# W1 loaded right behind batch 0 and scaled by three engines, batch 1's attention moved between the first MLP matmuls, g turned on TensorE

## The chip, the cores and the metric

One core of one Trainium2 chip runs the whole program. The metric is the device time of one execution in microseconds (us). The kernel before took 349.22 us as the median of three runs (346.89 to 353.25). Times below are medians of runs; positions inside a run are microseconds from the start of the profiled span, which is about 2 us shorter than the run's time.

## The reference, cut to what matters

```python
# 8 batches, 8 heads, 576 rows, 64 columns a head
A  = softmax(q @ q_or_k_landmarks); Bm = softmax(q_lm @ k_lm^T); C = softmax(q_lm @ k^T)   # 32 landmarks
Z  = Bm^T / (norm1 * norminf)
for _ in range(6):
    Z = 2 * Z - Z @ Bm @ Z              # "Newton's steps"
x  = (A @ Z @ C @ v)                    # attention's output, as rows of 512
xn = (x - mean) / sqrt(var + 1e-6) * g_ln
out = x + relu(xn @ w_ch1) @ w_ch2      # MLP, 512 -> 2048 -> 512
```

The kernel takes the g of the normalisation into W1: each row of W1 is multiplied by one element of g when it is brought to fp16. The rows of all batches are cut into 36 blocks of 128 and 9 groups of four blocks; the MLP runs group by group.

## The kernel before: the parts that matter here

All transfers go through one queue, in program order: batch 0's q, k, v, then g, batch 1's q and k, W1, batch 1's v, W2, and later the other batches. W1's and W2's fp32 pieces and the attention's output blocks share one pool of 16 buffers:

```python
xpool = ctx.enter_context(tc.tile_pool(name="xpool", bufs=16))
def scale_w1(i):                       # W1 in pieces of 256 columns
    for c in range(KCH):
        if c == 0: act(o, i_, AF.Copy, scale=g_sb[:, c:c + 1])      # ScalarE
        else:      pool.tensor_scalar(out=o, in0=i_, scalar1=g_sb[:, c:c + 1], ...)   # GpSimd
def fetch_w2():
    for m in range(MCH + 6):
        if m < MCH:
            w2_stg[m] = xpool.tile([P, DM], FP32, name="w2stg", tag="xblk")
            keep(nc.sync.dma_start(out=w2_stg[m][:], in_=moe_w_ch2[ts(m, P), :]))
        if m >= 6:
            pool.tensor_copy(out=w2_16[:, m - 6, :], in_=w2_stg.pop(m - 6)[:])
def x_of(j):                           # the buffer of output block j
    if j not in x_blk:
        x_blk[j] = xpool.tile([P, DM], FP32, name="xblk", tag="xblk")
    return x_blk[j]
```

The MLP is a generator; `fill(n)` issues its next n units (one to three matmuls each) between the steps of an attention. `a0` and `a1` are the attentions of batches 0 and 1. In the kernel before, batch 1's q and k steps run between Newton's steps of batch 0, and its later steps between the MLP's first matmuls:

```python
run(a0, a1, a0); warm(2, 256)          # warm: idle matmuls that keep TensorE's clock up
run(a0, a1, a0); warm(2, 256)
run(a0, a1, a0, a0)
scale_w1(0); run(a1); fill(1); run(a0); scale_w1(1); ...
for _ in a0: pass                      # the rest of batch 0's rows
run(a1); fill(10); cast_v(1)
fetch_w2()                             # W2 after batch 0's rows
...
for i, _ in enumerate(a1):
    fill(5 if i < 8 else 6); settle()
    cast_and_load(pairs[0], pairs[1])
    if 3 <= i < 11: pairs[0].next_job()    # VectorE's preparation of batches 2 and 3
```

The names in the profile: psb are the landmark scores, psn Newton's products, pszc the product after the last step, psy the output rows, xblk the blocks, psxt and xnT the turned activations, psh and pso the two MLP matmuls, natv the attention's values. Where a milestone is needed below I use four: the first psh, batch 1's pszc, the second half of the psb of batches 2 and 3 ("second psb"), and the end.

The softmax here doesn't subtract the row's maximum and nothing guards it: scores larger than these inputs give would overflow.

Of the kernel before, what the change touches and what calls it, by code (L numbers as in the profile page):

```python
# [9 lines left out]
FP16 = mybir.dt.float16  # L10
# [6 lines left out]
P = 128  # L17
# [3 lines left out]
def kernel(  # L21
# [67 lines left out]
    def load_qk(b):  # L89
        for u in range(U):  # L90
            raw[b]["q", u] = load(q, b, u, nc.sync)
            raw[b]["k", u] = load(k, b, u, nc.sync)
# [30 lines left out]
    keep(nc.sync.dma_start(out=g_sb[:], in_=moe_g_ln.rearrange("(c p) -> p c", p=P)))  # L123
# [6 lines left out]

# [56 lines left out]
    load_qk(1)  # L187
    for u in range(U):
        for nm in ("q", "k"):
            cast_qk(1, u, nm, pool)  # L190

    w1_16 = wpool.tile([P, KCH, HID], FP16, name="w1_16")
    w2_16 = wpool.tile([P, MCH, DM], FP16, name="w2_16")
    w1_src = moe_w_ch1.rearrange("(c p) f -> p c f", p=P)
    xpool = ctx.enter_context(tc.tile_pool(name="xpool", bufs=16))

    W1N = 256
    w1_stg = {}



    def load_w1(i):
        for half in range(2):
            stg = xpool.tile([P, DM], FP32, name="w1stg", tag="xblk")
            keep(nc.sync.dma_start(
                out=stg[:].rearrange("p (c f) -> p c f", c=2),
                in_=w1_src[:, 2 * half:2 * half + 2, ts(i, W1N)]))
            w1_stg[i, half] = stg

    def scale_w1(i):  # L210
        for c in range(KCH):
            o, i_ = w1_16[:, c, ts(i, W1N)], w1_stg[i, c // 2][:, ts(c % 2, W1N)]
            if c == 0:
                act(o, i_, AF.Copy, scale=g_sb[:, c:c + 1])
            else:
                pool.tensor_scalar(out=o, in0=i_, scalar1=g_sb[:, c:c + 1],
                                   scalar2=0.0, op0=ALU.mult, op1=ALU.add)

    for i in range(HID // W1N):
        load_w1(i)  # L220
# [463 lines left out]
    def by_act(j):  # L684
        return 4 <= j < 8 or 8 <= j < 28 and j % 2 == 0
# [3 lines left out]
    def block_done(j):  # L689
# [3 lines left out]
        if g == 0:  # L693
            center_by_act(j)
            later.append(lambda: stats(j))
        elif g == 1:
            later.append(lambda: center_by_act(j))
        else:
            if by_act(j):
                later.append(lambda: stats_by_act(j))  # L700
            else:
                stats(j)
            later.append(lambda: center(j) if g <= mlp_at[0] + 1
                         else uncentered.setdefault(g, []).append(j))
# [27 lines left out]
    def center_by_act(j):  # L732
# [5 lines left out]
        if by_act(j):  # L738
            junk = mxn.tile([P, DM], FP16, name="junk", tag="junk", bufs=1)
            act(junk[:], x_blk[j][:], AF.Square, bias=negm[:],  # L740
                accum_out=mvgs[g][:, u, 1:2])
# [53 lines left out]
    def mlp():  # L795
        for g in range(NGRP):
            mlp_at[0] = g
            hT = mhT.tile([P, MCH, 512], FP16, name="hT", tag="hT")
            if g == 0:
                for u in (0, 2):  # L800
# [4 lines left out]
                    for m0 in range(0, MCH, 2):  # L805
# [3 lines left out]
                        if u == 0 and m0 < MCH - 6:  # L809
                            scale_w1(m0 // 2 + 3)  # L810
# [63 lines left out]
    def run(*who):  # L874
        for a in who:
            next(a)

    warm(80, 64)
    for _ in range(4):
        run(a0)  # L880
        warm(3, 256)
    run(a0)
# [4 lines left out]
    warm(4, 256)  # L887
    run(a0)
    warm(2, 256)
    run(a0)  # L890
    warm(2, 256)
    run(a0, a1, a0)
    warm(2, 256)
    run(a0, a1, a0)
    warm(2, 256)
    run(a0, a1, a0, a0)
    scale_w1(0)
    run(a1)
    fill(1)
    run(a0)  # L900
    scale_w1(1)
    fill(1)
    scale_w1(2)
    fill(4)
    run(a0)
    fill(4)
    for _ in a0:
        pass
    run(a1)
    fill(10)  # L910
    cast_v(1)
    fetch_w2()
    run(a1)
    fill(16)
# [12 lines left out]

    for i, _ in enumerate(a1):
        fill(5 if i < 8 else 6)
        settle()  # L930
        cast_and_load(pairs[0], pairs[1])
        if 3 <= i < 11:
            pairs[0].next_job()
    for _ in range(3):
        pairs[0].next_job()
# [48 lines left out]
```

## Time and profile before

| | before |
|---|---|
| time, us | 349.22 (346.89 to 353.25) |
| span of the profiled run | 346.7 |
| TensorE busy | 323.3, 93% |
| VectorE, ScalarE, GpSimd busy | 46%, 49%, 36% |
| first psh / batch 1's pszc / second psb | 29.22 / 54.58 / 74.17 |

The page's rows of busy tenths show where there is room. Each digit is 8.7 us; 9 means 90% or more.

```profile
PE 323.3 (93%) x3818; PEld 166.4 (48%) x3818; DVE 158.7 (46%) x341; ACT 168.6 (49%) x328; POOL 125.5 (36%) x199
...
PE   8875979879889999999999999999999999999994
...
PEclk9999999989999999999999999999999999999998
DMA  7999999999982281171012101210130031022023
```

Apart from the last slice, TensorE is below 9 only in the first twelve, 104 us, and the DMA engines are full in the same stretch. The clock is full but for two slices. After those twelve nothing but TensorE's matmuls counts.

This is how TensorE reaches its first MLP matmul in the kernel before (its timeline: start, duration, what, number of instructions, and in brackets the idle time before it with what ended that):

```profile
20.06 0.43 PE L73 MATMUL pss<-pm,nat 128*128 128x64 f16 x9 [1.49 <-issue]
...
22.85 0.24 PE L73 MATMUL pszc<-st,bm 32*32 32x64 f16 x8
...
29.22 1.03 PE L73 MATMUL psh<-xnT,w 128*128 128x256 f16 x8 [0.52 <-DVE xnT L67]
```

Waiting on "issue" is waiting on nothing that the profile can name.

### The profile page before, as it was taken

What the parts mean: (1) busy time and instruction counts of PE and PEld (TensorE: products, weight loads), DVE (VectorE), ACT (ScalarE), POOL (GpSimd) and SP (SyncE); (2) the same over time, 40 slices, a digit from 0 to 9 for tenths busy, and PEclk for the clock granted to TensorE, in tenths of its full rate; (3) what the DMA queues carried; (4) which work ended last, traced back from release to release, by engine and by line L of the source; (5) the groups of instructions that cost most, each with busy time, mean ns of one, the idle gap of its engine ahead of it and who ended that gap; (6) DMA issues with size and microseconds to landing.
All of it is one profiled execution on the core that took longest, in us unless ns stands there. A gap on an engine that the chain in (4) does not pass through costs nothing.

```text
span 346.7 us, 8948 instructions
## 1 busy us (share of the span) xinstructions
PE 323.3 (93%) x3818; PEld 166.4 (48%) x3818; DVE 158.7 (46%) x341; ACT 168.6 (49%) x328; POOL 125.5 (36%) x199
## 2 busy tenths in 40 slices
PE   8875979879889999999999999999999999999994
PEld 7553744435433545554445444544444454444441
DVE  2645629885499753346777402337850010020011
ACT  4359844943544595045738750465146226415600
POOL 2488878999953498047023000003120010000000
PEclk9999999989999999999999999999999999999998
DMA  7999999999982281171012101210130031022023
GB/s 274 357 353 362 344 404 369 233 384 317 236 281 91 62 260 47 32 201 32 2 30 64 31 2 42 55 30 2 34 84 6 15 77 32 0 62 61 0 54 69
DMA packets 21528, 46.72 MB, mean 135 GB/s; under 512 B 3056, under 2 KB 7152, under 8 KB 21488
## 3 DMA queue, kind: packets, MB, share of 16 engines
q1 hardware_dynamic: 21488, 46.15, 43.6%
q8 instruction: 30, 0.49, 0.6%
q14 instruction: 10, 0.08, 0.1%
HBM read 36.70 MB, written 9.44 MB: 133 GB/s over the span
## 4 chain that ended last, share of the span: by engine, by line
PE 75%; DVE 7%; DMA 7%; ACT 6%; issue 2%; SPq 1%; POOL 0%; DVEq 0%
PE psh L73 35%; PE pso L73 30%; DMA w1stg<-in_moe_w_ch_dram 4%; DMA g_sb<-in_moe_g_ln_dram 3%; PE pscv L73 3%; ACT xn L67 2%; PE psy L73 2%; PE psxt L77 2%; DVE st L67 2%; DVE xblk L67 2%; PE psn L73 1%; DVE xT L67 1%; ACT junk L67 1%; PE psea L73 1%; PE psec L73 1%
## 5 line engine op out<-in xcount | busy, mean ns | idle before, releaser
L73 PE MATMUL pso<-w,hT 128*128 128x512 f16 x576 | 137.6, 381 | 0.0
L73 PE MATMUL psh<-xnT,w 128*128 128x512 f16 (+1 forms) x640 | 133.7, 358 | 2.9 <-DVE xnT L67 1.2
L67 ACT ACTIVATE hT<-psh 128x512 f16<-128x512 f32 x144 | 85.3, 597 | 54.5 <-PE psh L73 54.3
L73 PEld LDWEIGHTS <-w 128*128 128x128 f16 x640 | 59.7, 98 | 60.6 <-issue 2.3
L73 PEld LDWEIGHTS <-hT 128*128 128x128 f16 x576 | 53.9, 98 | 55.7 <-issue 2.1
L67 DVE SCALAR_TENSOR_TENSOR ot<-pso,rstd,xblk 128x512 f32<-128x512 f32 x36 | 27.0, 749 | 107.7 <-PE pso L73 107.7
L67 ACT COPY xnT<-psxt 128x512 f16<-128x512 f16 x32 | 18.7, 584 | 59.1 <-PE psxt L77 59.0
L67 POOL CAST nat<-stg 128x1152 f16<-128x1152 f32 x28 | 31.8, 1147 | 5.1 <-DMA stg<-in_k_dram 1.8
L67 DVE TENSOR_TENSOR xblk<-psy,rcpd 128x512 f32<-128x512 f32 (+1 forms) x40 | 27.6, 691 | 1.8
L67 POOL TENSOR_SCALAR xn<-xblk,negm 128x512 f16<-128x512 f32 x18 | 12.5, 694 | 35.2 <-PE psxt L77 34.1
L67 DVE SCALAR_TENSOR_TENSOR st<-st,psn 128x384 f16<-128x384 f16 (+3 forms) x30 | 13.5, 450 | 24.2 <-PE psn L73 24.2
L67 POOL TENSOR_SCALAR xn<-xblk,mvg 128x512 f16<-128x512 f32 x10 | 6.9, 695 | 45.8 <-PE psxt L77 28.3
L67 POOL CAST natv<-stg 128x1152 f16<-128x1152 f32 x16 | 17.9, 1151 | 11.8 <-DMA stg<-in_v_dram 11.8
L67 DVE STREAM_TRANSPOSE xT<-nat 128x576 uint32<-128x576 uint32 x24 | 18.4, 767 | 4.8 <-POOL nat L67 3.5
L67 POOL TENSOR_SCALAR negm<-mvg 128x1 f32<-128x1 f32 x18 | 3.5, 192 | 37.6 <-PE psy L73 23.9
L73 PE MATMUL psy<-zcbd,ea 128*128 128x260 f16 (+1 forms) x80 | 16.0, 277 | 1.2 <-ACT xT L67 0.6
L77 PE MATMUL psxt<-ident,xn 128*128 128x128 f16 x144 | 14.2, 222 | 2.1 <-ACT xn L67 1.6
L67 DVE TENSOR_REDUCE lmk<-xT 128x64 f16<-128x1152 f16 x12 | 16.1, 1341 | 0.1
L67 POOL TENSOR_TENSOR asum<-asum 128x256 f32<-128x256 f32 (+2 forms) x30 | 15.0, 501 | 2.3
L67 DVE BATCH_NORM_STATS2 st<-xblk 128x6 f32<-128x512 f32 x22 | 15.2, 689 | 0.6
L77 PEld LDWEIGHTS <-xn 128*128 128x128 f16 x144 | 10.9, 99 | 9.1 <-ACT xn L67 2.0
L67 DVE RECIPROCAL rcpd<-psy 128x8 f32<-128x8 f32 (+1 forms) x40 | 8.0, 201 | 11.1 <-PE psy L73 10.6
(99 smaller groups left out, 257.6 us busy)
## 6 DMA issues: line engine op xcount, KB each, us to landing
stg<-in_q_dram SPq DMA_DIRECT2D x16, 576.0 KB, 6.9
stg<-in_k_dram SPq DMA_DIRECT2D x16, 576.0 KB, 7.8
out_dram<-ot SPq DMA_DIRECT2D x72, 128.0 KB, 2.4
stg<-in_v_dram SPq DMA_DIRECT2D x10, 576.0 KB, 8.2
w1stg<-in_moe_w_ch_dram SPq DMA_DIRECT2D x16, 256.0 KB, 6.0
w2stg<-in_moe_w_ch_dram SPq DMA_DIRECT2D x16, 256.0 KB, 5.2
stg<-in_v_dram SPq DMA_DIRECT2D x12, 288.0 KB, 8.7
g_sb<-in_moe_g_ln_dram SPq DMA_DIRECT2D x1, 2.0 KB, 10.1
```

What stands on the lines that cost most here:

```text
L67: return lambda *args, **kw: keep(getattr(self.engine, op)(*args, **kw))
L73: keep(nc.tensor.matmul(o, l, r, start=start, stop=stop, tile_position=(rb, cb), skip_group_check=(skip or cb != 0)))
L77: keep(nc.tensor.matmul(o, i_, idn, is_transpose=True, tile_position=(0, 0)))
```

## The change

Its intent: the MLP should start earlier and then run without gaps. W1 is loaded right behind batch 0's data in pieces of 512 columns and scaled by GpSimd, VectorE and ScalarE between Newton's steps; batch 1's whole attention moves behind the MLP's start, one step between every few MLP units; g arrives in four rows of 512 bytes and is turned by one TensorE matmul; group 1's statistics go from ScalarE partly to VectorE. W2's loads move ahead of batch 0's rows, and nine blocks are named before them, so that the blocks have their buffers first.

```diff
-    keep(nc.sync.dma_start(out=g_sb[:], in_=moe_g_ln.rearrange("(c p) -> p c", p=P)))
+    keep(nc.sync.dma_start(out=g_rows[:], in_=moe_g_ln.rearrange("(c p) -> c p", p=P)))
-    load_qk(1)                       # and its casts; W1 behind it in pieces of 256 columns
+    for f in range(HID // DM):
         for c in range(KCH):
+            w1_stg[f, c] = stg = xpool.tile([P, DM], FP32, name="w1stg", tag="xblk")
+            keep(nc.sync.dma_start(out=stg[:], in_=moe_w_ch1[ts(c, P), ts(f, DM)]))
+    load_qk(1)
     load_v(1)
... by_act, block_done: statistics of groups 0 and 1
-        if g == 0:
+        if g == 0 and u % 2 == 0:
             center_by_act(j)
             later.append(lambda: stats(j))
-        elif g == 1:
-            later.append(lambda: center_by_act(j))
+        elif g == 0:
+            stats(j)
+            ... dve.tensor_scalar(out=xn_of[j][:], in0=x_blk[j][:], ..., op0=ALU.subtract)
... the order of steps
-    for _ in range(4):
+    for i in range(4):
         run(a0)
         warm(3, 256)
+        if i == 2:
+            TR(psg[:], g_rows[:], ident4[:])
+            dve.tensor_copy(out=g_sb[:], in_=psg[:])
...
+    scale(pool, (0, 3), (1, 3), (2, 0), (2, 1), (2, 3), (3, 0), (3, 1), (3, 3))
+    for it, on_dve in enumerate(((0, 0), (0, 1), None, (1, 0), (1, 1), None)):
+        run(a0) ; scale(dve, on_dve) ; scale(scalar, ...) ; warm(2, 256)
...
+    for j in range(9):
+        x_of(j)
+    fetch_w2()
     run(a0)                          # batch 0's rows: block 0, block 1
...
+    ahead = [2, 2, 2, 3, 4, 4, 7] + 6 * [5] + [5, 4, 5, 5, 5, 5]
     for i, _ in enumerate(a1):
-        fill(5 if i < 8 else 6)
+        fill(ahead[i])
         settle()
-        if 3 <= i < 11: pairs[0].next_job()
+        if i >= 9:  cast_and_load(pairs[0], pairs[1])
+        if i >= 12: pairs[0].next_job()
+    while pairs[0].jobs:
+        pairs[0].next_job(); fill(4); cast_and_load(pairs[0], pairs[1])
```

More of the change, by code (lines that the diff above doesn't have):

```diff
@@ L122 @@
     g_sb = wpool.tile([P, KCH], FP32, name="g_sb")
-    keep(nc.sync.dma_start(out=g_sb[:], in_=moe_g_ln.rearrange("(c p) -> p c", p=P)))
+    g_rows = wpool.tile([KCH, P], FP32, name="g_rows")
+    keep(nc.sync.dma_start(out=g_rows[:], in_=moe_g_ln.rearrange("(c p) -> c p", p=P)))
     zeros = const.tile([P, 256], FP16, name="zeros")
@@ L129 @@
     make_identity(nc, ident16)
+    ident4 = const.tile([KCH, KCH], FP32, name="ident4")
+    nc.vector.tensor_copy(out=ident4[:], in_=ident16[0:KCH, 0:KCH])
     pm16 = const.tile([P, 64], FP16, name="pm16")
@@ L184, with scale_w1 @@
                 dve.tensor_copy(out=t[:, :, D], in_=(mask4t if i in (3, 5) else mask4)[:])
-    load_qk(1)
-    for u in range(U):
-        for nm in ("q", "k"):
-            cast_qk(1, u, nm, pool)
     w1_16 = wpool.tile([P, KCH, HID], FP16, name="w1_16")
     w2_16 = wpool.tile([P, MCH, DM], FP16, name="w2_16")
-    w1_src = moe_w_ch1.rearrange("(c p) f -> p c f", p=P)
     xpool = ctx.enter_context(tc.tile_pool(name="xpool", bufs=16))
-    W1N = 256
     w1_stg = {}
-    def load_w1(i):
-        for half in range(2):
-            stg = xpool.tile([P, DM], FP32, name="w1stg", tag="xblk")
-            keep(nc.sync.dma_start(
-                out=stg[:].rearrange("p (c f) -> p c f", c=2),
-                in_=w1_src[:, 2 * half:2 * half + 2, ts(i, W1N)]))
-            w1_stg[i, half] = stg
-    def scale_w1(i):
-        for c in range(KCH):
-            o, i_ = w1_16[:, c, ts(i, W1N)], w1_stg[i, c // 2][:, ts(c % 2, W1N)]
-            if c == 0:
-                act(o, i_, AF.Copy, scale=g_sb[:, c:c + 1])
-            else:
-                pool.tensor_scalar(out=o, in0=i_, scalar1=g_sb[:, c:c + 1],
-                                   scalar2=0.0, op0=ALU.mult, op1=ALU.add)
-    for i in range(HID // W1N):
-        load_w1(i)
+    for f in range(HID // DM):
+        for c in range(KCH):
+            w1_stg[f, c] = stg = xpool.tile([P, DM], FP32, name="w1stg", tag="xblk")
+            keep(nc.sync.dma_start(out=stg[:], in_=moe_w_ch1[ts(c, P), ts(f, DM)]))
+    def scale_w1(f, c, engine):
+        o, i_ = w1_16[:, c, ts(f, DM)], w1_stg.pop((f, c))[:]
+        if engine is scalar:
+            act(o, i_, AF.Copy, scale=g_sb[:, c:c + 1])
+        else:
+            engine.tensor_scalar(out=o, in0=i_, scalar1=g_sb[:, c:c + 1],
+                                 scalar2=0.0, op0=ALU.mult, op1=ALU.add)
+    load_qk(1)
     load_v(1)
@@ L684, in by_act @@
     def by_act(j):
-        return 4 <= j < 8 or 8 <= j < 28 and j % 2 == 0
+        return 4 <= j < 28 and j % 2 == 0
     rstds = {}
@@ L692, in block_done @@
             mvgs[g] = mstat.tile([P, 4, 2], FP32, name="mvg", tag="mvg")
-        if g == 0:
+        if g == 0 and u % 2 == 0:
             center_by_act(j)
             later.append(lambda: stats(j))
-        elif g == 1:
-            later.append(lambda: center_by_act(j))
+        elif g == 0:
+            stats(j)
+            xn_of[j] = mxn.tile([P, DM], FP16, name="xn", tag="xn")
+            dve.tensor_scalar(out=xn_of[j][:], in0=x_blk[j][:], scalar1=mvgs[0][:, u, 0:1],
+                              scalar2=None, op0=ALU.subtract)
         else:
@@ L737, in center_by_act @@
         act(xn[:], x_blk[j][:], AF.Identity, bias=negm[:], scale=1.0)
-        if by_act(j):
-            junk = mxn.tile([P, DM], FP16, name="junk", tag="junk", bufs=1)
-            act(junk[:], x_blk[j][:], AF.Square, bias=negm[:],
-                accum_out=mvgs[g][:, u, 1:2])
     def center(j):
@@ L808, in mlp @@
                             yield True
-                        if u == 0 and m0 < MCH - 6:
-                            scale_w1(m0 // 2 + 3)
                         psh = psM.tile([P, 2, 256], FP32, name="psh", tag="pm")
@@ L872, with run, scale @@
     a0, a1 = attention((0,)), attention((1,))
-    def run(*who):
-        for a in who:
-            next(a)
+    def run(a):
+        next(a)
+    def scale(engine, *pieces):
+        for f, c in pieces:
+            scale_w1(f, c, engine)
     warm(80, 64)
-    for _ in range(4):
+    for i in range(4):
         run(a0)
         warm(3, 256)
+        if i == 2:
+            psg = psM.tile([P, KCH], FP32, name="psg", tag="pm")
+            TR(psg[:], g_rows[:], ident4[:])
+            dve.tensor_copy(out=g_sb[:], in_=psg[:])
     run(a0)
@@ L887 @@
     warm(4, 256)
+    scale(pool, (0, 3), (1, 3), (2, 0), (2, 1), (2, 3), (3, 0), (3, 1), (3, 3))
+    for it, on_dve in enumerate(((0, 0), (0, 1), None, (1, 0), (1, 1), None)):
+        run(a0)
+        if on_dve:
+            scale(dve, on_dve)
+        if it in (1, 3, 5):
+            scale(scalar, (it // 2, 2))
+        warm(2, 256)
     run(a0)
     warm(2, 256)
-    run(a0)
-    warm(2, 256)
-    run(a0, a1, a0)
-    warm(2, 256)
-    run(a0, a1, a0)
-    warm(2, 256)
-    run(a0, a1, a0, a0)
-    scale_w1(0)
-    run(a1)
+    for u in range(U):
+        for nm in ("q", "k"):
+            cast_qk(1, u, nm, pool)
+    cast_v(1)
+    for j in range(9):
+        x_of(j)
+    fetch_w2()
+    run(a0)
+    run(a0)
     fill(1)
+    scale(scalar, (3, 2))
+    fill(5)
     run(a0)
-    scale_w1(1)
-    fill(1)
-    scale_w1(2)
     fill(4)
     run(a0)
-    fill(4)
-    for _ in a0:
-        pass
-    run(a1)
-    fill(10)
-    cast_v(1)
-    fetch_w2()
-    run(a1)
-    fill(16)
+    settle()
+    run(a0)
     settle()
@@ L926, in cast_and_load @@
             (c if c.loads else after).next_load()
+    ahead = [2, 2, 2, 3, 4, 4, 7] + 6 * [5] + [5, 4, 5, 5, 5, 5]
     for i, _ in enumerate(a1):
-        fill(5 if i < 8 else 6)
+        fill(ahead[i])
         settle()
+        if i >= 9:
+            cast_and_load(pairs[0], pairs[1])
+        if i >= 12:
+            pairs[0].next_job()
+    while pairs[0].jobs:
+        pairs[0].next_job()
+        fill(4)
         cast_and_load(pairs[0], pairs[1])
-        if 3 <= i < 11:
-            pairs[0].next_job()
-    for _ in range(3):
-        pairs[0].next_job()
     counts = [[5, 5, 12, 12, 12, 12, 5, 5, 3, 3, 3, 3, 4] + 3 * [4] + 7 * [9]]
```

## The prediction

> **What bounds the kernel now.** I read the page's busy shares first (TensorE 93%, VectorE 46%), then the chain of work that ended last, then the engines' busy time in stretches of 5 us, then the order of instructions around each stretch where TensorE has gaps. From about 110 us to the end TensorE is full (the stretches show 9.7 to 10 of 10 us), so whatever the change does before 110 us reaches the end one to one, and nothing after it can absorb or add much. The early chain:
>
> ```profile
> 3.97 10.05 DMA g_sb<-in_moe_g_ln_dram
> 14.06 9.32 DMA w1stg<-in_moe_w_ch_dram
> 23.39 4.76 DMA w1stg<-in_moe_w_ch_dram
> 28.16 0.49 ACT w L67
> 28.65 1.00 ACT xT L67
> 29.65 0.64 ACT xn L67 x2
> ```
>
> The columns are start, duration, what. The chain says that W1 arrives late; this is what the change attacks. But the order of instructions shows a second arrival at the same moment: the first MLP matmul (psh) starts at 29.22 and its last releaser is the turned activation, 0.42 us at 28.74; W1's piece was scaled at 28.65. So W1 earlier alone buys about half a microsecond; the activation's own chain has to shorten too.
>
> The stretches (us; then PE, PEld, DVE, ACT, POOL busy, granted clock, DMA share, GB/s):
>
> ```profile
> 25.00:30.00 5.00, 2.90 (x38) 2.26 (x38) 2.88 (x7) 4.53 (x9) 4.61 (x11) 1.00 1.10 349
> 30.00:35.00 5.00, 3.27 (x29) 2.27 (x27) 2.64 (x7) 4.94 (x13) 4.23 (x8) 1.00 1.07 371
> 50.00:55.00 5.00, 3.24 (x43) 1.98 (x44) 4.37 (x7) 1.21 (x3) 4.04 (x4) 1.00 1.02 408
> 55.00:60.00 5.00, 5.00 (x26) 2.28 (x25) 4.84 (x10) 2.15 (x5) 4.09 (x4) 1.00 1.04 363
> 60.00:65.00 5.00, 4.59 (x43) 2.11 (x41) 4.93 (x10) 4.83 (x12) 4.61 (x7) 1.00 1.03 230
> 65.00:70.00 5.00, 4.11 (x47) 2.06 (x48) 3.85 (x6) 4.90 (x14) 4.69 (x8) 1.00 1.02 240
> 70.00:75.00 5.00, 2.44 (x57) 1.09 (x55) 4.31 (x9) 1.50 (x4) 4.31 (x5) 0.95 1.02 388
> 75.00:80.00 5.00, 5.00 (x129) 2.67 (x111) 3.99 (x12) 1.78 (x3) 4.60 (x8) 0.71 1.03 392
> ```
>
> ScalarE is full from 25 to 35; VectorE is nearly full from 50 to 75, and TensorE has holes there: that is the other limit. VectorE's groups from 50.6 to 74.2 name the work, and TensorE's waits from 29 to 75 its price:
>
> ```profile
> L67 DVE STREAM_TRANSPOSE xT<-nat 128x576 uint32<-128x576 uint32 x8 | 6.2, 770 | 3.5 <-POOL nat L67 3.5
> L67 DVE TENSOR_REDUCE lmk<-xT 128x64 f16<-128x1152 f16 x4 | 5.3, 1334 | 0.0
> L67 DVE TENSOR_REDUCE lmq<-xT 128x64 f16<-128x1152 f16 x2 | 2.7, 1348 | 0.0
> ...
> PE psn L73 <- DVE st L67: 2.1, 1, 2.1
> PE psb L73 <- DVE lmq L67: 2.0, 2, 1.2
> ```
>
> These 14 jobs prepare batches 2 and 3 (14.5 us with the two lmq transposes). TensorE's second half of their psb matmuls at 74.17 waits for the last of them.
>
> **What the Trainium skill says.** "DMA: Bandwidth & Descriptors", section "Queues, rings and completion order": each engine consumes a ring's descriptors in ring order. The trace agrees: all transfers come from one queue, batch 0's pieces land in order at 4.5, 6.0, 8.6, 10.1, 12.1 and 13.7 us, and g, issued at 3.97 just behind v, lands at 14.06. The section "Why a DMA increments its semaphore by 16 and not by 1" says that the number of engines follows from the slowest dimension, so g in four rows uses four engines instead of 16; no run here shows that yet. It means four larger descriptors, but still behind v in those rings. "VectorE: DVE Perf Modes", section "Mode 2×_2P — use both read ports for one tensor", gives fp32 tensor_scalar from SBUF two results a cycle, as for copies; the trace's cast of 1152 fp32 in 760 ns (0.66 ns each) agrees with a double rate.
>
> **The change part by part.**
>
> *W1 behind batch 0, in 2 KB rows.* Batch 0 ends at 13.7. A 262 KB piece at the trace's 350 to 400 GB/s takes 0.7 to 0.75 us: the 16 pieces land from about 14.4 to 25.5, instead of to about 31. GpSimd has 8 x 0.69 = 5.5 us instead of 24 x 0.48 = 11.5; ScalarE 4 pieces of about 0.65 instead of 8 x 0.49; VectorE 4 of about 0.4 (estimate from the cast), in the 0.4 to 0.5 us gaps that Newton's steps leave. W1 then gates nothing. Batch 1's q and k land behind it, at about 27.5 to 33, v at 36, and W2 to 46 or so, about as now because the bytes to there are the same.
>
> *g turned on PE.* The turn stands in TensorE's program order before the fourth q/k step, which now runs at 10.9. By the ring order g lands at about 13.3 to 13.7. So TensorE stands there 2.5 us. Of it 0.25 comes back, because batch 0's value product already waits that long for v. Newton then starts at about 18.3 instead of 15.96.
>
> *Batch 1 out of batch 0's way.* Newton's six steps and the next stage took 15.96 to 22.85 = 6.9 us, with one 2.4 us wait of VectorE in which TensorE did batch 1's work. Alone they take 6 x 0.87 = 5.2, some 5.4 with the scaling. The last product is then at 23.7 (now 22.85). Behind it: zcbd 1.2, psy and reciprocal, block 0 at +2.5, block 1 at +3.4, its statistics 0.8 and subtraction 0.4 on VectorE, turning and copying 0.8: first MLP matmul at +5.5, so about 29.2, against 29.22 now. Without the g wait it would be 26.8.
>
> *Batch 1 inside the MLP.* Its four q/k steps, now before 29, cost TensorE about 1.15 each with gaps, 4.6 us behind the MLP's start. The wait of its second step for a PSUM buffer that VectorE frees after group 0's late statistics costs some 2 us more. In exchange disappear most of the gaps between 29 and 53 (about 5 us in the windows: 1.7 in 30 to 35, 2.1 at 50 where a job stood before Newton's update). From the start to batch 1's last Newton step: 24.0 now, about 26.5 after. That step is at 53.2 now, and then at 53.3 (no g wait) to 56.
>
> *The jobs for batches 2 and 3.* Now they begin at 50.6, between Newton's steps; then only at the last one. VectorE has behind it jobs 14.5, five rows 5 x 0.9 = 4.5, zcbd 0.9, three outputs 2.2, plus new statistics for two blocks of group 1, 1.7: 24.1, some 22.6 with the overlap now seen (24 us of records in 22.4). So the psb at 74.17 moves to 76 to 78.6: 2 to 4.5 us later. It stands at nearly the same place in the MLP stream: 127 units of fill before it now (36 + 70 + 5 + 16), 126 after (10 + 83 + 28 + 5).
>
> *ScalarE's chain for group 1* (its 8 us from 60 to 68) goes: 4 x about 2.3 us become 2 x 1.7 on ScalarE and 3 us on GpSimd. That frees an engine that in this stretch is not the one TensorE waited for longest.
>
> *Later.* Between 74 and 110 TensorE idles about 3 us and lost 1.5 us to a clock of 0.71 in 75 to 80 (5 x 0.29). If it comes later to the same places, 1 to 2 us of this can go. Sum: +2 to +4.5, less 1 to 2: about +1.5 us by the working.
>
> **The rivals.** (1) *The intended gain.* g lands in time (four rows only, nothing in the rings ahead), the MLP starts at 26.8, and the filled gaps and the relieved ScalarE count in full: 11 us of TensorE gaps between 29 and 110 shrink to 5 or 6. Then 340 to 344. For it: the fill numbers look tuned to arrivals; ScalarE is 97% busy from 60 to 70 now. Against it: VectorE's 22 us of work before that psb. (2) *VectorE binds fully*, the g wait is full, and nothing is recovered: 353 to 356. (3) *Only trading*: start earlier, the same work moved behind it, all gaps alike: 348 to 350.
>
> **Range and chances.** My working gives 350.7; because the hand-set fill numbers speak for rival 1, I put it at 350.0. The time before itself spread from 346.89 to 353.25. Range 342.5 to 356. Faster by over 2% (below 342.2) 0.13, within 2% 0.73, slower (above 356.2) 0.14.
>
> **What would show it.** In the changed profile: g's landing and a wait of TensorE ahead of psg near 11 to 13.5; first psh near 29 (rival 1: under 27); W1's pieces all scaled before 27; TensorE nearly without gaps from 30 to 53; the first xT of batches 2 and 3 after 53 rather than 50.6; VectorE full from there and the second psb at 76 or later. I am wrong if g lands by 11, or if that psb comes before 73.

## The result

The changed kernel is correct and took 367.57 us (366.46 to 369.57, four runs) beside 348.58 us for the kernel before (346.89 to 353.25, four runs, of which the one of 353.25 counts as slow): a ratio of 1.0557, with a 95% interval of 1.0486 to 1.0627. It is 5.6% slower, where I had predicted 350.0 us and a range that ended at 356. A ratio here is the mean time of one kernel's fast runs over that of the other's fast runs of the same rounds, so it is not quite the ratio of the medians that I quote.

The page of the changed kernel, the rows that answer to those shown of before:

```profile
PE 327.0 (90%) x3825; PEld 168.5 (46%) x3825; DVE 163.8 (45%) x353; ACT 160.2 (44%) x306; POOL 123.3 (34%) x189
...
PE   7770569986889899999999999999999999999994
...
PEclk9685599999999999999999999999999999999999
DMA  7999997044997636316201300220022022022013
```

A slice is 9.1 us here. The fourth slice, 27 to 36 us, has a busy share of 0 on TensorE, and the clock is at 0.5 in it and in the next one. That hole was in no part of my prediction.

TensorE's timeline of the changed kernel shows the hole and the milestones:

```profile
12.95 0.24 PE L77 MATMUL psg<-ident,g_rows 4*128 4x4 f32 x1 [2.68 <-DMA g_rows<-in_moe_g_ln_dram]
...
26.75 1.20 PE L73 MATMUL psy<-zcbd,ea 128*128 128x260 f16 x4
39.29 0.61 PE L77 MATMUL psxt<-ident,xn 128*128 128x128 f16 x4 [11.34 <-ACT xn L67]
...
41.54 1.86 PE L73 MATMUL psh<-xnT,w 128*128 128x256 f16 x8 [0.52 <-DVE xnT L67]
...
68.05 0.24 PE L73 MATMUL psn<-st 32*32 32x64 f16 x8
69.42 0.24 PE L73 MATMUL pszc<-st,bm 32*32 32x64 f16 x8
...
91.11 0.22 PE L73 MATMUL psb<-lmk,lmq 32*32 32x32 f16 x6 [0.53 <-DVE lmq L67]
...
98.67 0.52 PE L73 MATMUL pscv<-natv,ecT 32*32 32x65 f16 x45 [1.30 <-issue]
...
104.32 0.20 PE L73 MATMUL pscv<-natv,ecT 32*32 32x65 f16 x1 [1.76 <-issue]
```

psy at 26.75 makes the first two output blocks. The activation made from them is turned only at 39.29, after 11.34 us. The releaser named is ScalarE's xn; ScalarE in turn waits for the block. So the question goes to VectorE, which writes the block. Its timeline:

```profile
27.56 0.21 DVE L67 RECIPROCAL rcpd<-psy 128x8 f32<-128x8 f32 x1 [0.47 <-PE psy L73]
37.03 0.69 DVE L67 TENSOR_TENSOR xblk<-psy,rcpd 128x512 f32<-128x512 f32 x1 [9.27 <-POOL w L67]
37.64 0.20 DVE L67 RECIPROCAL rcpd<-psy 128x8 f32<-128x8 f32 x1
37.93 0.69 DVE L67 TENSOR_TENSOR xblk<-psy,rcpd 128x512 f32<-128x512 f32 x1
```

The same two steps in the kernel before, without any wait between them:

```profile
24.39 0.21 DVE L67 RECIPROCAL rcpd<-psy 128x8 f32<-128x8 f32 x1 [0.36 <-PE psy L73]
24.68 0.69 DVE L67 TENSOR_TENSOR xblk<-psy,rcpd 128x512 f32<-128x512 f32 x1
```

In the changed kernel the reciprocal is done at 27.77, and the write of block 0 starts 9.27 us later. Nothing of its data is missing; its inputs are psy and that reciprocal. What released it is a GpSimd instruction that writes w. GpSimd's timeline tells which:

```profile
31.72 1.15 POOL L67 CAST nat<-stg 128x1152 f16<-128x1152 f32 x1 [0.36 <-DMA stg<-in_k_dram]
33.22 1.15 POOL L67 CAST natv<-stg 128x1152 f16<-128x1152 f32 x1 [0.36 <-DMA stg<-in_v_dram]
34.73 1.15 POOL L67 CAST natv<-stg 128x1152 f16<-128x1152 f32 x1 [0.35 <-DMA stg<-in_v_dram]
35.82 10.35 POOL L67 CAST w<-w2stg 128x512 f16<-128x512 f32 x16
```

W is here W2: the casts of its 16 pieces begin at 35.82, at 0.65 us each, behind the casts of batch 1's q, k and v, which follow their transfers. VectorE was released when the second cast was done, at about 37.0. A buffer that held a piece of W2 was handed to block 0. In the built program (seen in its allocations, not in a trace) block 0 has the same address as W2's second piece, and blocks 1 to 8 those of the next eight. The line `x_of(j)` for nine blocks ahead of `fetch_w2()` was written to prevent just this, and did not: naming a tile that nothing had written yet reserved nothing.

The stretches of 5 us (PE, PEld, DVE, ACT, POOL busy, granted clock, DMA share, GB/s) show what was running meanwhile:

```profile
25.00:30.00 5.00, 2.72 (x24) 1.02 (x24) 1.82 (x6) 0.00 (x0) 3.12 (x3) 0.53 1.05 395
30.00:35.00 5.00, 0.00 (x0) 0.00 (x0) 0.00 (x0) 0.00 (x0) 3.72 (x4) 0.50 1.05 389
35.00:40.00 5.00, 0.61 (x4) 0.34 (x4) 2.77 (x6) 2.06 (x4) 4.89 (x8) 0.50 1.05 387
```

TensorE, VectorE and ScalarE do nothing at all from 30 to 35. The clock stays at 0.50 until about 46 us, and the first eight psh matmuls took 1.86 us instead of 1.03. The Trainium skill's page "TensorE: Matmul & The Clock Gate", section "Part 1: The HAM clock gate (the "warmup" mystery)", says that TensorE runs at half its clock after about 3.4 us without work and needs as long of work to get it back. This trace agrees with that in part. The half clock lasted through the hole and ended at 45.8, 4.3 us after the first psh. But it had begun at 25.3, before the hole: the stretch from 20 to 25.3 has a clock of 1.00, and TensorE's last matmuls ahead of the hole ended at 27.95. TensorE's longest idle time between 20 and 25.3 was 1.10 us, so no wait of that length began it; the run with more idle matmuls comes back to this.

The four milestones split the 18.1 us by which the span grew:

| stretch | before | after | difference | predicted |
|---|---|---|---|---|
| start to first psh | 29.22 | 41.54 | +12.3 | 0 |
| to batch 1's last Newton product | 24.0 | 26.5 | +2.5 | +2.5 |
| from there to the second psb | 20.95 | 23.06 | +2.1 | +1.6 |
| from there to the end | 272.5 | 273.7 | +1.2 | -1 to -2 |

(The last product is at 53.22 before and 68.05 after.) Two rows of four came out near what had been worked out beforehand, though the second partly by luck, as the last part shows. The first row is the error; the last has the wrong sign.

### The profile page after: what moved, and what is told of

It is laid out like the page before. It is cut to its first block, busy times and chain, and to the rows that moved or that the text cites. A ratio compares the mean times of both kernels' runs of the same rounds, so it can differ in the third digit from the quotient of the medians.

```text
span 364.8 us, 8945 instructions
## 1 busy us (share of the span) xinstructions
PE 327.0 (90%) x3825; PEld 168.5 (46%) x3825; DVE 163.8 (45%) x353; ACT 160.2 (44%) x306; POOL 123.3 (34%) x189
## 4 chain that ended last, share of the span: by engine, by line
PE 72%; DMA 12%; DVE 11%; issue 2%; POOL 1%; SPq 1%; ACT 0%; DVEq 0%; POOLq 0%
PE psh L73 34%; PE pso L73 28%; DMA stg<-in_v_dram 5%; DMA w1stg<-in_moe_w_ch_dram 3%; PE pscv L73 2%; DMA stg<-in_q_dram 2%; DVE st L67 2%; DVE xblk L67 2%; DVE xT L67 2%; PE psxt L77 2%; PE psy L73 2%; DMA w2stg<-in_moe_w_ch_dram 1%; DVE lmk L67 1%; PE psn L73 1%; DVE ot L67 1%
## 5 line engine op out<-in xcount | busy, mean ns | idle before, releaser
L73 PE MATMUL psh<-xnT,w 128*128 128x512 f16 (+1 forms) x640 | 135.5, 362 | 0.6 <-DVE xnT L67 0.5
L67 DVE TENSOR_TENSOR xblk<-psy,rcpd 128x512 f32<-128x512 f32 (+1 forms) x40 | 27.6, 691 | 11.0 <-POOL w L67 9.3
L67 POOL TENSOR_SCALAR xn<-xblk,mvg 128x512 f16<-128x512 f32 x12 | 8.4, 696 | 65.9 <-PE psxt L77 28.4
L67 POOL TENSOR_SCALAR xn<-xblk,negm 128x512 f16<-128x512 f32 x20 | 13.9, 696 | 35.7 <-PE psxt L77 34.3
L67 DVE BATCH_NORM_STATS2 st<-xblk 128x6 f32<-128x512 f32 x24 | 16.6, 692 | 0.7
L67 ACT ACTIVATE junk<-xblk 128x512 f16<-128x512 f32 x12 | 7.6, 630 | 13.8 <-DVE xblk L67 13.8
```

Of the source, the lines that this page charges most:

```text
L67: return lambda *args, **kw: keep(getattr(self.engine, op)(*args, **kw))
L73: keep(nc.tensor.matmul(o, l, r, start=start, stop=stop, tile_position=(rb, cb), skip_group_check=(skip or cb != 0)))
```

## The experiments

Twelve kernels ran. They were measured in four groups, each with its own runs of the kernel before. Where two calls are compared, the kernel before of the same call is the yardstick, because its own median moved from 347.16 us (11 runs) to 351.09 (4 runs) between two calls, and single runs of it reach from 345.97 to 357.11. Positions and spans in the table below are of one profiled execution each. Two theories stood at the start. Theory A: the buffer of block 0 is the main loss, and the wait for g the second. Theory B: the early part only hides a loss that comes from VectorE's jobs after 50 us anyway, so mending the start gives little.

| run | median us | ratio to before (95%) | first psh | batch 1's pszc | second psb | span |
|---|---|---|---|---|---|---|
| before | 348.58 | 1 | 29.22 | 54.58 | 74.17 | 346.7 |
| the change | 367.57 | 1.0557 (1.0486 to 1.0627) | 41.54 | 69.42 | 91.11 | 364.8 |
| W2 later | 359.21 | 1.0339 (1.0277 to 1.0402) | 31.2 | 60.18 | 81.87 | 356.9 |
| g later | 368.23 | 1.0591 (1.0522 to 1.066) | 41.3 | 69.24 | 90.93 | 364.6 |
| both | 354.53 | 1.0191 (1.0116 to 1.0265) | 27.9 | 58.01 | 79.70 | 353.9 |
| blocks touched | 358.96 | 1.0323 (1.0248 to 1.0398) | 31.4 | 59.98 | 81.67 | 354.7 |
| both, jobs earlier | 352.08 | 1.0031 (0.9908 to 1.0153) | 27.4 | 57.65 | 75.35 | 350.7 |
| both, statistics later | 353.77 | 1.0088 (0.9992 to 1.0184) | 27.7 | 56.75 | 78.45 | 352.1 |
| both, more idle matmuls | 355.05 | 1.0044 (0.9801 to 1.0287) | 27.8 | 56.91 | 78.60 | 353.6, slow |
| these three together | 351.17 | 1.002 (0.9908 to 1.0132) | 27.5 | 56.01 | 73.71 | 349.4 |
| and fill, and one step moved | 348.98 | 1.0015 (0.9972 to 1.0058) | 27.5 | 55.21 | 73.25 | 346.6 |

The runs from "jobs earlier" to "these three together" are of the call in which before had its 351.09.

### W2's loads behind batch 0's rows

```diff
     for j in range(9): x_of(j)
-    fetch_w2()
     run(a0)
     run(a0)
     ...
     run(a0); settle()
+    fetch_w2()
```

> The changed kernel with one line moved: W2's 16 loads and casts are written behind batch 0's rows instead of ahead of them. Theory A (buffers): block 0's write stood from 27.77 to 37.03 because its buffer was given first to a W2 piece, which GpSimd casts only behind batch 1; then block 0 is written near 27.8, the first psh falls from 41.5 to about 32, and the run loses 9 to 10.5 us: 356 to 359 by the clock that says 367.6 now. Rival B (arrival): GpSimd's order and the DMA queue hold that point anyway, and moving W2 leaves the first psh at 38 or later: 364 to 368. Rival C (VectorE's later jobs absorb it): the first psh moves to 32, but the second psb of batches 2 and 3 stays near 91: under 3 us gained.

Measured: 359.21 us, 8.4 us less than the change's 367.57 (the ratios to before, 1.0339 and 1.0557, say the same). The first psh came at 31.2. The buffer wait of block 0 is gone. Theory B falls with it: the second psb moved by 9.2 us along with the first psh.

### The nine blocks touched, W2's loads left where the change has them

This run tells the buffer from the place of the loads: one column of each named block is written, nothing else moves.

```diff
     for j in range(9):
-        x_of(j)
+        dve.memset(x_of(j)[:, 0:1], 0.0)
     fetch_w2()
```

> The changed kernel with one edit: the nine block tiles that are named ahead of W2's loads get a one-column memset on VectorE each, so that they really take their buffers first; W2 is still loaded at the same place, ahead of batch 0's rows. Theory A (naming a tile reserves nothing, the order of the first writes does): block 0 no longer waits for GpSimd's cast of W2, the first MLP matmul comes at 30-32 instead of 41.5, and the whole comes within 0.5% of the run that moved W2's loads (ratio 1.028-1.040). Theory B (what hurts is that W2 is asked for so early, whatever buffers it takes): first MLP matmul still after 38, ratio 1.05 or more.

Measured: 358.96 us, ratio 1.0323, the same as moving the loads. VectorE's timeline of this run:

```profile
26.46 0.18 DVE L67 MEMSET xblk<- 128x1 f32 x9
26.99 0.21 DVE L67 RECIPROCAL rcpd<-psy 128x8 f32<-128x8 f32 x1 [0.34 <-PE psy L73]
27.23 0.69 DVE L67 TENSOR_TENSOR xblk<-psy,rcpd 128x512 f32<-128x512 f32 x1
```

Nine writes of 59 ns, 0.18 us in all as they overlap, and block 0 follows its reciprocal at once where it had waited 9.27 us. So theory A holds in its sharper form: a buffer of this pool whose block has been named but not written is handed on, and W2's loads took it. In the built program of this run none of W2's pieces has the address of one of the nine blocks. By the medians, the change is 8.6 us faster with this one line.

### g's turn three steps later

```diff
-        if i == 2: TR(psg[:], g_rows[:], ident4[:]); dve.tensor_copy(out=g_sb[:], in_=psg[:])
     run(a0); warm(2, 256); run(a0); warm(3, 256)
+    TR(psg[:], g_rows[:], ident4[:]); dve.tensor_copy(out=g_sb[:], in_=psg[:])
```

> The changed kernel with g turned on TensorE three steps later, behind batch 0's scores, where g has long landed; W2 stays where it is. TensorE's 2.7 us wait ahead of psg goes. Theory A: batch 0's chain comes 2 to 2.7 us sooner to block 0, but that write still waits for the second W2 cast near 37, so nothing is gained: 366 to 368. Rival B (the g wait counts in full although W2 is in the way): 364.5 to 365.5.

Measured: 368.23 us, no gain, though psg now ran at 13.7 without a wait. VectorE's line of block 0 says why:

```profile
36.73 0.69 DVE L67 TENSOR_TENSOR xblk<-psy,rcpd 128x512 f32<-128x512 f32 x1 [12.60 <-POOL w L67]
```

Block 0 could have been written 3.6 us earlier than in the change (24.1 instead of 27.8), and waited 12.60 us instead of 9.27 for the same cast on GpSimd.

### Both

> Both moves together. Theory A: with the buffer free the g wait is on the path, so this is 2 to 3 us below the run with W2 alone moved: 353.5 to 356.5, first psh at 29 to 30. It stays above the kernel before (348.6), because batch 1's work and VectorE's late jobs remain: 4 to 7 us of it. Rival (the g wait was always hidden): no difference to W2 alone. Rival (everything but the buffer was a gain): below 348.

Measured: 354.53 us. Now g is worth 4.7 us over "W2 later" alone: the first psh moved from 31.2 to 27.9. Two waits that stand one behind the other cannot be added: the earlier one shows its price only when the later one is gone. Still, the kernel is 1.9% slower than before, although its MLP starts 1.3 us sooner. TensorE's waits from 26 to 80 us in this run (us in total, times, longest):

```profile
PE pst L77 <- DVE xblk L67: 4.3, 2, 3.5
PE psxt L77 <- ACT xn L67: 2.2, 1, 2.2
PE psb L73 <- DVE lmq L67: 2.2, 2, 1.6
```

The first line is batch 1's q and k turns, which wait for a PSUM buffer until VectorE, behind group 0's statistics, has read an output block. From the last Newton product (56.64) to the second psb (79.70) it again takes 23.06 us, exactly as in the change, with VectorE working through the jobs. The next three runs take this apart.

### Group 1's statistics alone, in the kernel before

```diff
-        return 4 <= j < 8 or 8 <= j < 28 and j % 2 == 0
+        return 4 <= j < 28 and j % 2 == 0
-        elif g == 1:
-            later.append(lambda: center_by_act(j))
```

> The kernel before with only the statistics of group 1 changed as the change has them: two blocks by ScalarE and GpSimd, two by VectorE and GpSimd, in place of four by ScalarE. My step said that ScalarE was not what TensorE waited for longest there: within 1 us of before (347.6 to 349.6), VectorE 1.7 us fuller. Rival 1 (ScalarE's chain from 60 to 68 was the limit): 2 to 4 us faster. Rival 2 (VectorE binds there fully): up to 1.7 us slower.

Measured: 348.84 us, ratio 1.0032 (0.9971 to 1.0093), span 346.9 against 346.7. This way of relieving ScalarE there brings nothing, though ScalarE was 97% busy from 60 to 70 us in the kernel before. It doesn't show that ScalarE was no limit: in this run TensorE waits 4.3 us for GpSimd's xn at 67.42, a wait that the kernel before doesn't have, and the clock is at 0.50 from 65 to 70. One wait was traded for another.

### "Both", with the casts from step 6 and the jobs from step 8 of batch 1

```diff
-        if i >= 9:   cast_and_load(pairs[0], pairs[1])
-        if i >= 12:  pairs[0].next_job()
+        if i >= 6:   cast_and_load(pairs[0], pairs[1])
+        if i >= 8:   pairs[0].next_job()
```

> The run with both moves (W2 later, g later; 354.5), and the 12 casts for batches 2 and 3 written from batch 1's 7th step instead of its 10th, their 14 VectorE jobs from its 9th step instead of its 13th. Theory (VectorE binds up to the second psb): 4.2 us of jobs move into Newton's steps, where VectorE idles about 1 us of each 1.4, and the second psb falls from 79.7 to 76 or 77: 3 to 4 us gained, 350.5 to 351.5. Rival 1 (TensorE's own order binds there, not VectorE): no change, 353.5 to 355.5. Rival 2 (jobs delay Newton's updates by as much as they save): 353 to 356.

Measured: 352.08 us, ratio 1.0031. VectorE's first job starts at 50.95 instead of 57.14, the second psb comes 4.35 us earlier, and the span is 3.2 us shorter than in "both". It is not the whole 4.35 because fewer MLP units (16 fewer) now stand ahead of that psb; they still have to run. From batch 1's last Newton product to the second psb it is now 19.06 us instead of 23.06, so VectorE's jobs did set that stretch. How much of the 3.2 us of span is theirs is not shown. The profiled execution of "both" has three stops of TensorE that no wait explains, 1.09 us at 19.49 and the two shown here, 3.55 in sum. This one has 0.39 us at 18.93 and the 0.60 shown here. That is about 2.6 us of the 3.2. First "both", then this run:

```profile
87.58 0.52 PE L73 MATMUL pscv<-natv,ecT 32*32 32x65 f16 x45 [0.70 <-issue]
90.73 0.74 PE L73 MATMUL pscv<-natv,ecT 32*32 32x65 f16 x71
93.23 0.20 PE L73 MATMUL pscv<-natv,ecT 32*32 32x65 f16 x1 [1.76 <-issue]
```

```profile
82.05 0.53 PE L73 MATMUL pscv<-natv,ecT 32*32 32x65 f16 x46
83.18 0.30 PE L73 MATMUL pscv<-natv,ecT 32*32 32x65 f16 x26 [0.60 <-issue]
```

The medians, of four runs each, differ by 2.45 us, the ratios to before by 1.6%, with intervals of about 1% each way.

### "Both", with blocks 0, 2 and 3's statistics behind the last half block

```diff
-        elif g == 0:
-            stats(j); ...                      # at once, ahead of the next block's write
+        elif g == 0 and u == 1:  center_by_dve(j)
+        elif g == 0:             later.append(lambda: center_by_dve(j))
...
-    run(a0); settle(); run(a0); settle()
+    run(a0); run(a0); settle()
```

> The run with both moves, and VectorE writes batch 0's last half block before the statistics of blocks 0, 2 and 3 instead of after them. TensorE stood 3.46 us before batch 1's second turning, for a PSUM buffer that this half block frees. Theory (that wait is on the path and also costs clock, 0.50 from 38.3 to 41.6): 3 to 5 us gained, 349.5 to 351.5. Rival (hidden by the arrival of batch 1 or by VectorE's jobs later): 353.5 to 355.

Measured: 353.77 us; batch 1's pszc came 1.3 us earlier and the span is 1.8 us shorter than in "both" (0.9 us of it are shorter stops on "issue", 2.65 against 3.55 in sum). By the median it is 0.8 us, under the 3 to 5 expected. The PSUM wait of TensorE fell, and another took part of its place: 2.2 us for ScalarE's copies.

### "Both", with 24 more idle matmuls around Newton's steps and batch 0's rows

```diff
-        warm(2, 256)                  # after each Newton step
-    run(a0); warm(2, 256)
+        warm(2 if it < 2 else 4, 256)
+    run(a0); warm(4, 256)
...
-    run(a0); run(a0); fill(1)
+    run(a0); run(a0); warm(14, 256); fill(1)
```

> The run with both moves, and 26 more idle matmuls of 256 columns: two more behind each of Newton's last four steps and behind the last product, 14 between batch 0's first rows and the turning of block 0, where TensorE stands 2.2 us. Theory (the clock of 0.50 from 21.7 to 31.5 comes from thin work of TensorE and costs 2 us in group 0's first matmuls): the clock stays at 1.00 there, 1.5 to 3 us gained, 351.5 to 353. Rival 1 (the clock has another cause): still 0.50 and 0 to 1.5 us lost. Rival 2 (batch 1's wait behind it absorbs what is gained): clock 1.00, but 354 to 355.

The edit adds 24 idle matmuls (four times 2, 2 and 14), not the 26 of the text above. This one is inconclusive in time: two of its four runs, the profiled one among them, count as slow; ratio 1.0044 with an interval of 0.9801 to 1.0287. What it does show is the clock. From 20 to 30 us, first "both", then this run:

```profile
20.00:30.00 10.00, 6.52 (x54) 3.59 (x54) 6.39 (x16) 2.97 (x6) 7.63 (x10) 0.57 1.03 371
```

```profile
20.00:30.00 10.00, 8.05 (x86) 5.66 (x85) 7.51 (x18) 3.38 (x6) 6.58 (x9) 1.00 1.02 371
```

The clock went from 0.57 to 1.00 with 24 idle matmuls, and batch 1's pszc came 1.1 us earlier. The fast run of the three together, which has the same idle matmuls, is at 1.00 in this stretch too. In the kernel before it was 1.00 with batch 1's q and k steps there. That taking these steps out is what lost the clock fits this, but no run puts them back alone.

### The three together

> The run with both moves and the three further ones together (jobs earlier, statistics later, more idle matmuls). If the three causes are separate, the gains add up to 7 to 11 us: 343.5 to 347.5, level with the kernel before (347 to 348.6) or up to 1% below it. If one wait takes the place of another (VectorE is behind both the statistics and the jobs), 4 to 6 us: 348.5 to 350.5.

Measured: 351.17 us, ratio 1.002. The second psb is at 73.71, for the first time ahead of the kernel before (74.17). The median lies just above the 348.5 to 350.5 of the second expectation, 3.4 us below "both" (1.7% by the ratios). Of the change's 18.1 us of span 15.4 are undone (349.4 against 364.8), 2.0 of them by shorter stops on "issue" (2.2 in sum against 4.2). TensorE's first wait on the list from 26 to 80 us is shown here; two waits for VectorE's lmq sum to 2.2 us as well:

```profile
PE pst L77 <- ACT xT L67: 2.2, 1, 2.2
```

ScalarE's copies of batch 1's turns stood behind the logarithm of group 0's variances, which waited for the last statistics.

### That logarithm in batch 1's step 6, and more MLP units between the steps

```diff
-        if u == 3:
+        if u == 3 and g:
             later.append(lambda: deviations(g))
...
         fill(ahead[i]); settle()
+        if i == 6: deviations(0)
-    ahead = [...] + [5, 4, 5, 5, 5, 5]        counts = [[5, 5, 12, ...
+    ahead = [...] + [5, 4, 5, 12, 5, 5]       counts = [[14, 5, 12, ...
```

> Everything of the run with the pool, the jobs, the statistics and the idle matmuls mended, and two more edits. Theory A (what is left of the loss is MLP work that no longer lies between the steps of batch 1 where VectorE binds, plus ScalarE's copies standing behind the logarithm of group 0's denominators): moving those to batch 1's own steps takes about 2 us from the last Newton step, and ten to twenty more MLP units between batch 1's steps fill TensorE's waits there; the span comes to 344-347 us and the ratio to before to 0.985-0.995, 1 to 2% below the run without the two edits. Theory B (the order of the first 80 us is by now worth nothing, since TensorE's work sets the whole): within 0.5% of the run without them, 349-351.

Measured: 348.98 us beside 348.71 (ratio 1.0015, 0.9972 to 1.0058, five rounds); the span is 346.6 against 346.7. The step from "these three" is -2.8 us in span, 0.8%, somewhat under the 1 to 2% expected, and the hoped-for 0.5 to 1.5% below before is not there. The first psh is 1.7 us and the second psb 0.9 us earlier than before; the end is not. TensorE's timeline tells where this went:

```profile
82.50 0.54 PE L73 MATMUL pscv<-natv,ecT 32*32 32x65 f16 x47
85.90 0.29 PE L73 MATMUL pscv<-natv,ecT 32*32 32x65 f16 x25 [2.86 <-issue]
```

TensorE stops for 2.86 us in the middle of 72 alike matmuls, and no wait explains it. Earlier, at 49.50, it also waited 3.0 us for one of VectorE's Newton updates, where the kernel before waited 2.1.

### The same extra fill in the kernel before

```diff
             while c.jobs:
                 c.next_job(); c.next_job()
-                fill(8)
+                fill(13)
```

> The kernel before with nothing but fill(8) made fill(13) in the loop that runs while jobs are left. If the extra MLP units are a gain that the old kernel could have had as well, it falls by 1 to 2 us (ratio 0.994-0.997), by as much as TensorE waits between batch 1's steps there. If the units only change places, ratio 0.998-1.002. If they hold up batch 1's own chain, ratio above 1.003.

Measured: 349.84 us beside 348.71, ratio 1.0035 (0.9976 to 1.0094): no gain. It, too, shows the odd stop, 2.58 us in the middle of a run of pscv at 86.25. The old kernel had not missed a gain that shows in the time. The comparison is not quite clean, since the stops on "issue" over 0.7 us sum to 4.1 us in this run's profile and to 2.6 in that of the kernel before.

### What the odd stops are: the kernel before with its instructions shifted

In the trace of each run one DMA queue, named "instruction", carries 30 packets of 16 KB. TensorE has some 7,650 records (each matmul and each weight load is one), 255 for each packet. I counted TensorE's records in order of their starts and looked where the stops of over 0.7 us fall that no wait explains. In all runs up to then they begin behind record 705, 1473, 2241, 2497, 2753 or 3009, which are all 193 modulo 256, and each ends 2.2 to 2.8 us after the start of one of those packets. The stop that ends at 20.06 in the kernel before is at record 705, as is one of 1.10 us that ends at 23.45 in the change; the two that end at 98.67 and 104.32 in the change are at 2241 and 2497, and the one that ends at 85.90 above is at 2497. (The "within 2" of the expectation came from a pause at record 1727; the profile does name a wait for that one, psy for VectorE's block, 1.55 us, and it is left out here.) The theory: TensorE fetches its instructions in blocks of 256, and a block that is asked for too late stops it. The run puts 66 more idle matmuls, 132 more instructions, ahead of everything, in the same time.

```diff
-    warm(80, 64)
+    warm(146, 35)
```

> The kernel before with 146 idle matmuls of 35 columns at the start instead of 80 of 64: about the same time on TensorE before the first data, and 132 more TensorE instructions ahead of everything else. Theory A (the stalls of TensorE that no wait explains are instruction blocks of 256 that come late; each stall of over 0.7 us that no wait explains, in the runs so far, began at a record whose number was 193 or within 2 of it, modulo 256): the stalls stay at these numbers and therefore move to other matmuls, into denser stretches of small ones, and the time rises by 2 to 8 us, ratio 1.006-1.023. Theory B (these stalls belong to the matmuls before which they stand): the stalls stay ahead of the same pss and psea matmuls, and the ratio is 0.997-1.003.

Measured: the stops are at records 705, 2753 and 3009 again, but now in front of other matmuls (TensorE's timeline):

```profile
17.73 0.34 PE L73 MATMUL pscv<-natv,ect 64*32 64x65 f16 x9 [2.50 <-issue]
...
92.33 0.31 PE L73 MATMUL pscv<-natv,ecT 32*32 32x65 f16 x15 [3.28 <-issue]
...
100.72 1.25 PE L73 MATMUL psh<-xnT,w 128*128 128x512 f16 x5 [1.29 <-issue]
```

They sum to 7.1 us where the kernel before has 2.6 us (1.49 and 1.10). The theory that these stops belong to certain matmuls falls. That they stand at block limits and each ends at a like distance from a packet's start speaks for late instruction blocks; no run changes the fetch itself. The size in time is less certain: 351.91 us beside 347.64, ratio 1.0072 with an interval of 0.9972 to 1.0173, so the median points to the low end of what was expected, and the interval does not exclude nothing. The profiled run counts as slow, so I use its positions and not its span.

The stops also change how the spans above are to be read. Those over 0.7 us sum to 2.6 us in the kernel before, 4.2 in the change, 3.6 in "both", nothing with the jobs earlier, 2.6 with the statistics later, 2.2 in the three together and 4.0 in the last version. So differences of 1 to 3 us between these single profiled spans are not the edits' alone.

## Why the prediction was wrong

**What bounds the kernel.** Right: 16.9 of the 18.1 us by which the span grew had arisen at the second psb, and the stretch from there to the end took nearly as long as before (273.7 against 272.5).

**g turned on TensorE.** Right: a stand of 2.5 us was predicted, and 2.68 came; g landed at about 12.9, between v's two landings at 11.97 and 13.44, as the ring order had suggested. The trace also has the four packets of 512 bytes that four rows should give; they start between 11.2 and 12.1.

**W1 in wide pieces.** Right in its consequence: all pieces but one were scaled by about 26 us and W1 gates nothing (the last, at 39.14, stands behind the hole). VectorE's pieces were mis-sized: 0.47 to 0.51 us, and 0.87 for the one that began 0.11 us after a piece of GpSimd's, where I had put 0.4. Where VectorE had begun first, it was GpSimd's piece that took longer, 0.83 and 0.86 instead of 0.69. The skill's page "SBUF — State Buffer", section "Who interferes with whom", says that such an operation of VectorE takes a port pair that GpSimd needs too, and one of the two then waits. The 0.87, 0.83 and 0.86 fit that; no run separates it.

**"Batch 1 out of batch 0's way".** This is the step that failed: "block 0 at +2.5, block 1 at +3.4 ... first MLP matmul at +5.5, so about 29.2". The last Newton product came at 25.86 instead of 23.7. That part has two terms that I had left out: Newton started 1.3 us late (19.63), the clock having been at 0.50 from 11.7 to 18.5, and 1.1 us was one of the stops on "issue". But the large one is "+2.5": block 0 was done at +11.9 (37.72), because its buffer had to be given back by a cast of W2 on GpSimd, behind batch 1's casts. I had accounted for engines and transfers in that step and not for buffers, and had taken the nine `x_of` calls for a reservation. With the blocks touched it is +2.6 for block 0 and +6.1 for the first psh (25.29, 27.92 and 31.4), close to the chain that I had predicted. This one term is 8 to 9 us of the time in two independent runs, and without it the change stands at about 1.03, still above my range. The working had smaller errors beside it. With the blocks touched, the four stretches of the table are longer than before by 2.2, 3.2, 2.1 and 0.5 us, 8.0 in sum, where it had 0, 2.5, 1.6 and -1 to -2. These 5 to 6 us are spread over the late start of Newton's steps, the waits behind the MLP's start and the last stretch.

**Batch 1 inside the MLP.** The size was right, 26.5 us predicted and 26.5 measured, but partly by luck: it was measured behind the hole, which the working did not have. Without the hole the stretch took 27.2 us (blocks touched), 27.6 (W2 later) and 28.7 ("both"). The wait for a PSUM buffer, put at 2 us, was 4.3 us in "both".

**The jobs.** Right: 22.6 us predicted from the last Newton step to the second psb, 23.06 measured, and 23.06 once more in "both". (The terms add up to 23.8, not to the 24.1 that stands there.) Moving the jobs back brought the second psb 4.0 us nearer to the last product, which confirms that VectorE binds in this stretch.

**"Later ... 1 to 2 us of this can go".** Wrong in sign: this stretch took 1.2 us longer. By arithmetic its stops on "issue" cover that: 1.30 and 1.76 against 1.10 in the kernel before, 1.96 us more. Without these it would be 0.8 us shorter, near what I had said; no run takes them out.

**A reading of before that I would correct.** I took the 2.4 us wait of VectorE at 20.74 for TensorE doing batch 1's work. 1.49 us of it was the stop at record 705.

**The intended gain.** These versions do not show it. With the buffer, g, the jobs, the statistics, the clock and the logarithm mended, the best version reaches the kernel before and no more. In its profile it starts its MLP 1.7 us sooner, leads by 0.9 us at the second psb, and the instruction stop there costs 1.76 us more than that of before. What stays open: whether a version with its block limits laid into the large matmuls would be faster than before; none was tried. Nor was any part of the change, such as the wide W1 pieces, tried alone in the kernel before, but for group 1's statistics. I also cannot say from these runs why the fetch is late in some blocks and not in others.

## What to carry to other kernels

When a change moves a load or an allocation, ask of every buffer in a shared pool who had it last and which engine's queue gives it back; in this kernel a tile that was only named held nothing, and a one-column write settled it. Waits in series hide one another, so undo suspects in pairs and not only alone. An engine that is "free" in a stretch may be what keeps the clock, and a saving early in a kernel counts only if the next limit, here VectorE's jobs and TensorE's own instruction supply, moves with it.

## What the Trainium skill lacked or had wrong

- "Runtime: NRT & Kernel Launch", section "Instruction fetch mechanics", calls the cost of crossing a block of 256 instructions mostly hidden. That fits most of the 30 packets of a run. But in the kernel before, the change and the shifted kernel TensorE stopped at two or three such limits for 1.10 to 3.28 us at a time, always at the same record numbers modulo 256, 2.2 to 2.8 us after a packet of that queue had started; they sum to 2.6 us in the kernel before and to 4.2 us in the changed one (1.10, 1.30, 1.76). Around each of these five stops the DMA engines' share was 1.00 to 1.08 and TensorE ran many small matmuls; one of the shifted kernel's, of 1.29 us, fell at a share of 0.48. The page has the size of a block right.
- No page that I read says that a pool's buffer is handed on while its tile is named but not written. Here that was worth 8.6 us: 367.57 against 358.96 us by nine memsets of 59 ns.
- "TensorE: Matmul & The Clock Gate" does not say how much work in a window is enough to keep the clock, and these runs do not settle it. In "both" the clock was 0.57 from 20 to 30 us while TensorE's records show it 65% busy, though with few and small matmuls; 24 more idle matmuls brought it to 1.00.
